# Combine rows kept in DRAM, two more weight slots, larger raw tiles, and a longer lead-in of idle products in a fused attention, soft mixture and feed-forward kernel

## The chip, the cores and the metric

The kernel runs on one core of a Trainium2 chip. The metric is device time in microseconds for one execution; lower is better. TensorE is called PE below, VectorE DVE, ScalarE ACT, GpSimd POOL, and SyncE, which issues most DMAs here, SP.

## What is computed

Three stages follow each other, all in float32 with a tight tolerance: causal attention with a cumulative bias (4 batches, 8 heads, 576 tokens, head width 64), a soft mixture of 8 experts over 2304 tokens, and a feed-forward block of width 2048.

```python
# attention, per head
cum = np.cumsum(np.maximum(s, 0.0), axis=-1)
scores = scale * q @ k.T + np.minimum(-(cum[:, None] - cum[None, :]), 0.0)   # causal mask
attn = softmax(scores);  x = attn @ v
# soft mixture: x is 2304 x 512
logits = x @ phi                                  # 2304 x 32 slots
slot_in = softmax(logits, axis=0).T @ x           # 32 x 512
slot_out[e] = relu(slot_in[e] @ w1[e]) @ w2[e]    # 8 experts, 4 slots each
c = softmax(logits, axis=1)                       # the combine rows
x = c @ slot_out
# feed-forward
h = x @ w_in
g = where(h >= 1, h, where(h <= -1, 0, (h + 1) ** 2 / 4))
out = g @ w_out
```

## The kernel before

**Attention.** The 32 heads are taken in 16 pairs, `pi`. The score rows of a pair are cut into row blocks `t`, and these into four groups `g` (`GROUPS`). For each group, `s_mm` makes the scores on PE in two steps: products of the raw q and k (tile `x`), and then products of the bias rows (tile `ext`, bf16). `maxima` takes masked row minima on DVE, `exps` the exponentials on ACT, `transp` transposes the result on PE, `evac_p` copies it out, and `pv` multiplies by v. Nothing is reordered by a scheduler: a list `plan` of (time, function) pairs is sorted once, and its order is the program order of every engine. One pair takes 12 units of plan time (`PLAN`, `GATE`, `PRE_AT` hold positions in it).

**Lead-in.** Before the first pair, DVE makes the running sum of s and splits it into three bf16 parts (tile `part`). ACT writes constant rows into `ext[0]` and `ext[1]` (line 255, four instructions each), and four small DMAs bring `part` into `ext[0]` (`ext_rows`, line 238, two issued by SP, two by ACT). `N_IDLE` = 7 products of the zeroed tile `ext[1]` with itself keep PE busy meanwhile (line 251). After each group of four pairs, that is, after each batch, `gate_parts` computes the softmaxes of the mixture; `c3` and `c3_tail` transpose the combine weights into 96 rows (value, value, rest) per token.

**Combine rows.** All 2304 columns of those rows stand in one SBUF tile, `cstack` (96 x 2304, 9 KB per partition), until the feed-forward stage reads them in blocks of 384 tokens.

**Weights.** The 64 parts of 512 KB of `w1` and `w2` are loaded into slots of 4 KB per partition. `slots` makes them: 16 "post" and `N_LEFT` = 12 "pre" slots exist from the start, and `PRE_AT` gives the 28 plan positions at which one load each is issued. When attention's own tiles are closed (`heads.close()`), 6 more "pre" and `N_TMP[0]` = 7 "tmp" slots come from their space, and 4 more when the last softmaxes are done. All later loads wait for a slot that an expert gives back (`release`). SP issues them in the order of `LOADS`. In the same stage `c3` of batch 2 and the softmaxes of batch 3 run.

**Raw tiles.** During attention, `w_in` (float64 in two int32 halves) is converted to float32 in chunks of 256 columns. `get` fetches one chunk of 256 KB (rows of 2 KB) into one of three tiles `st`; POOL (lines 665, 666) and DVE (690, 678) convert it.

**Feed-forward.** `h_part` multiplies a block of combine rows by `mst` (the slot outputs already multiplied by `w_in`), ACT and DVE make the activation and split it, and `o_part` makes nine products of 128x512 per unit. The very first product on combine rows is at line 1069.

## Time and profile before

| | |
|---|---|
| median of three runs | 453.62 us (453.22 to 454.09) |
| profiled execution, its own time | 454.85 us |
| its span, first to last instruction | 453.0 us |
| PE busy | 438.7 us, 97% |
| ACT, DVE, POOL busy | 338.2, 297.6, 57.2 us |
| HBM read, written | 66.93 MB, 6.93 MB |

The span is what the views of the trace show. The 1.85 us between it and the execution's own time lie around it. Busy time of PE is modelled from pipelined products, so that a full PE need not be at its peak.

### The profile page before, as it was taken

How to read it: one execution, taken by the hardware profiler on the slowest of the kernel's cores; microseconds unless marked ns; L12 is line 12 of the kernel's file. 1: busy time of each engine (PE TensorE's matmuls, PEld its weight loads, DVE VectorE, ACT ScalarE, POOL GpSimd, SP SyncE). 2: the span in 40 equal slices, each digit the busy share in tenths (PEclk: the TensorE clock that was granted, in tenths of full speed). 3: DMA queues.
4: the chain of work that ended last, by engine and by line, in shares of the span. 5: the costliest groups of instructions: out<-in, count | busy, mean ns of one | idle time of the engine just before them, and what ended most of it. 6: DMA issues, size and time to landing. Idle time of an engine off the chain costs nothing.

```text
span 453.0 us, 11875 instructions
## 1 busy us (share of the span) xinstructions
PE 438.7 (97%) x4406; PEld 335.3 (74%) x4406; DVE 297.6 (66%) x908; ACT 338.2 (75%) x916; POOL 57.2 (13%) x188
## 2 busy tenths in 40 slices
PE   8799999999999999998999999999999999999996
PEld 3577766776767677666666888888888888888884
DVE  5798988988898866300179897866555555545552
ACT  5899998998999895322379898976777767676772
POOL 2233413431430121000010000000000000000000
PEclk9999999999999999999999999999999999999999
DMA  3999898998787689899895550003001001001002
GB/s 80 245 278 249 250 260 258 279 290 212 211 225 232 176 263 302 300 398 408 302 375 213 200 192 17 0 2 140 1 0 69 1 0 71 1 1 71 0 1 70
DMA packets 30428, 75.24 MB, mean 166 GB/s; under 512 B 4514, under 2 KB 7138, under 8 KB 30370
## 3 DMA queue, kind: packets, MB, share of 16 engines
q1 hardware_dynamic: 30214, 74.34, 51.9%
q8 instruction: 35, 0.57, 0.5%
q14 instruction: 23, 0.19, 0.1%
q10 hardware_dynamic: 156, 0.14, 0.1%
HBM read 66.93 MB, written 6.93 MB: 163 GB/s over the span
## 4 chain that ended last, share of the span: by engine, by line
PE 91%; ACT 3%; DVE 3%; DMA 1%; issue 1%; SPq 0%; POOL 0%; ACTq 0%; POOLq 0%
PE o L992 14%; PE o L994 14%; PE o L993 13%; PE s L311 10%; PE s L422 8%; PE s L380 7%; PE s L457 4%; PE hp L960 3%; PE p L816 3%; PE p L785 3%; PE s L319 3%; PE s L414 3%; PE s L550 1%; PE s L739 1%; DVE g L974 1%
## 5 line engine op out<-in xcount | busy, mean ns | idle before, releaser
L992 PE MATMUL o<-wt,gh 128*128 128x512 f32 x288 | 113.0, 393 | 0.1
L993 PE MATMUL o<-wt,gh 128*128 128x512 f32 x288 | 112.1, 389 | 0.0
L994 PE MATMUL o<-wt,gl 128*128 128x512 f32 x288 | 112.1, 390 | 0.0
L370 ACT ACTIVATE P<-s,nm 128x256 f32<-128x256 f32 (+4 forms) x160 | 85.8, 557 | 10.5 <-DVE nm L325 9.6
L976 ACT CAST gh<-g 128x384 fp32r<-128x384 f32 x95 | 48.8, 514 | 48.6 <-DVE g L974 46.2
L982 DVE TENSOR_TENSOR gl<-g,gh 128x384 fp32r<-128x384 f32 x95 | 53.1, 559 | 40.8 <-ACT gh L976 40.7
L325 DVE CUSTOM_DVE_ANT_0 s<-s,tri 128x256 f32<-128x256 f32 (+4 forms) x160 | 73.8, 507 | 8.8 <-PE s L311 5.4
L974 DVE SCALAR_TENSOR_TENSOR g<-w,hp 128x384 f32<-128x384 f32 x95 | 52.5, 552 | 32.4 <-ACT w L965 31.9
L992 PEld LDWEIGHTS o<-wt,gh 128*128 128x128 f32 x288 | 54.2, 188 | 12.5 <-issue 1.5
L994 PEld LDWEIGHTS o<-wt,gl 128*128 128x128 f32 x288 | 54.1, 188 | 12.3 <-DVE gl L982 0.5
L993 PEld LDWEIGHTS o<-wt,gh 128*128 128x128 f32 x288 | 54.2, 188 | 7.6
L311 PE MATMUL s<-x 64*128 64x512 f32 (+3 forms) x256 | 56.5, 468 | 0.1
L964 ACT ACTIVATE w<-hp,half 128x384 f32<-128x384 f32 x95 | 54.8, 577 | 1.1 <-PE hp L916 1.1
L965 ACT ACTIVATE w<-w 128x384 f32<-128x384 f32 x95 | 49.9, 525 | 3.0
L406 ACT COPY pts<-s 128x384 f32<-128x384 f32 (+2 forms) x125 | 47.2, 471 | 0.8
L380 PE MATMUL s<-ident,P 64*128 64x64 f32 x800 | 42.3, 226 | 2.3 <-ACT P L370 2.2
L380 PEld LDWEIGHTS s<-ident,P 64*128 64x128 f32 x800 | 36.6, 139 | 10.4 <-issue 3.5
L370 ACT ACTIVATION_READ_ACCUMULATOR P<-s,nm 128x1 f32 x160 | 37.8, 236 | 0.0
L422 PE MATMUL s<-pts,v 128*64 128x512 f32 (+3 forms) x256 | 37.3, 433 | 0.1
L960 PE MATMUL hp<-cstack,mst 96*128 96x384 f32 x95 | 32.2, 340 | 1.1 <-DVE cv L177 0.9
L175 DVE TENSOR_SCALAR wt<-wt 128x512 int32<-128x512 int32 x20 | 9.1, 453 | 36.4 <-DMA wt<-in_w_out_dram 36.4
L311 PEld LDWEIGHTS s<-x 64*128 64x128 f32 x256 | 28.9, 193 | 4.8 <-issue 2.1
(177 smaller groups left out, 560.4 us busy)
## 6 DMA issues: line engine op xcount, KB each, us to landing
wt<-in_w_dram SPq DMA_DIRECT2D x64, 512.0 KB
x<-in_qkT_dram SPq DMA_DIRECT2D x32, 288.0 KB
wt<-in_w_out_dram SPq DMA_DIRECT2D x16, 512.0 KB
st<-in_w_in_dram SPq DMA_DIRECT2D x24, 256.0 KB
out_dram<-ob SPq DMA_DIRECT2D x17, 256.0 KB
v<-in_v_main_dram SPq DMA_DIRECT2D x16, 256.0 KB
w_in_f<-wif SPq DMA_DIRECT2D x4, 512.0 KB
wt<-w_in_f SPq DMA_DIRECT2D x4, 512.0 KB
```

Of the source, the lines that this page charges most:

```text
L311: T.matmul(out=o[h][:, off:off + n], lhsT=y[r, 0, c:c + 128], rhs=y[r, 1, 0:n], start=(k == 0), stop=(k == 1))
L325: V.tensor_tensor_reduce(out=sc, in0=sc, in1=mask[:, mask.shape[1] - n:], scale=-1.0 / SCALE, scalar=init, op0=ALU.add, op1=ALU.min, accum ...
L370: A.activation(out=out_, in_=in_, func=AF.Exp, bias=nm, scale=-1.0, accum_out=sm[:, k:k + 1])
L380: T.transpose(out=o[f][:, c:c + 64], in_=P[r], identity=ident[r, r])
L422: T.matmul(out=o[r, 128 * j:512], lhsT=vt[:, j, r], rhs=pts_t[pi][:, h, 512 * j:384 * j + 512], start=(j == 0), stop=(j == 3))
L964: A.activation(out=w, in_=hp, func=AF.Relu, bias=half, scale=0.5)
L965: A.activation(out=w, in_=w, func=AF.Square)
L974: V.scalar_tensor_tensor(out=g, in0=w, scalar=1.0, in1=hp, op0=ALU.min, op1=ALU.max)
L982: V.tensor_tensor(out=gl, in0=g, in1=gh.bitcast(F32), op=ALU.subtract)
L992: hh = lambda t: T.matmul(out=o_t[j][t], lhsT=gh[:, r[t]], rhs=wh[c], start=(c == 0), stop=False)
L993: hl = lambda t: T.matmul(out=o_t[j][t], lhsT=gh[:, r[t]], rhs=wl[c], start=False, stop=False)
L994: lh = lambda t: T.matmul(out=o_t[j][t], lhsT=gl[:, r[t]], rhs=wh[c], start=False, stop=(c == 15))
```

## The change

Six edits stand in one diff.

1. The lead-in has 15 idle products of 128x384 instead of 7 of 128x512. They read the mask tile `tri`, still zero in the columns used, and its memset moves ahead of that of `ext[1]` on POOL.
2. Fourteen more idle products (`WARM_0`: 5 of 128x384, 3 and 6 of 128x256) are put into the first pair: before the first transposes, between the transposes of its two heads, and after the scores of its last group.
3. In the first pair, the minima of group 1 are taken head by head.
4. The combine rows of a batch go into one tile `c_st` (96 x 576) and from there to DRAM (`c4`): by SP for batches 0 and 1, by ACT for batches 2 and 3. `c_load` brings them back in blocks of 384 tokens: blocks 0 and 1 just behind the one-element DMA `gate`, the others during the feed-forward stage. `idphi` moves from the lasting tiles to attention's own.
5. The space makes one more "pre" slot (13) and one more "tmp" slot (8). `PRE_AT` gets 29 positions, wider apart in the first two thirds of attention and closer in the last.
6. A raw tile holds two chunks (512 KB, rows of 4 KB). There are two such tiles, and each is asked for when the tile before the last has been read.

```diff
-N_IDLE = 7
+N_IDLE = 15
+WARM_0 = (5, 3, 6)
-N_LEFT = 12
+N_LEFT = 13
-N_TMP = (7, 4)
+N_TMP = (8, 4)
-PRE_AT = [3 * int(5 + 2.2 * _n) + 0.76 for _n in range(24)] + [171.76, 177.76, 183.76, 186.76]
+PRE_AT = [3 * int(5 + 2.55 * _n) + 0.76 for _n in range(19)] + [3 * int(52.3 + 1.1 * _n) + 0.76 for _n in range(10)]
 GATE = dict(
-    ... c3=27.64,
+    ... c3=27.64, c4=30.77,
...
-    cstack = const.tile([96, NTOK], F32R, name="cstack")
+    c_st = const.tile([96, S], F32R, name="c_st")
+    c_dram = w_dram.tile([96, NTOK], F32, name="c_rows")
...
                 nc.sync.dma_start(out=gate[0:1], in_=last[0:1, 0:1])
+                c_load(0, cs)
+                c_load(1, None)
...
-        stage = hpool("stage", 3)
+        stage = hpool("stage", 2)
...
         load_qk(0)
+        G.memset(tri, 0.0)
         G.memset(ext[1], 0.0)
...
-        idle = bank()
-        for _ in range(N_IDLE):
-            T.matmul(out=idle, lhsT=ext[1][:, 0, 0:128], rhs=ext[1][:, 0, 0:512], start=True, stop=True)
+        def idle_mm(out, n):
+            for _ in range(n):
+                T.matmul(out=out, lhsT=tri[:, 0:128], rhs=tri[:, 0:out.shape[1]], start=True, stop=True)
+        idle_mm(bank()[:, 0:384], N_IDLE)
...
+        idphi = hpool("idp", 1).tile([128, 4, D + NSLOT], F32, name="idphi")
...
+            if (pi, g) == (0, NG - 1):
+                idle_mm(o[0][:, 256:512], WARM_0[2])
...
-            for t, off in GROUPS[g]:
-                for k in heads_:
+            todo = [(k, *p) for p in GROUPS[g] for k in heads_]
+            for k, t, off in todo if pi else sorted(todo, key=lambda e: e[0]):
...
+            if (pi, g) == (0, 0):
+                idle_mm(o[0][:, 0:384], WARM_0[0])
...
+                if (pi, g, h) == (0, 0, 1):
+                    idle_mm(o[0][:, 256:512], WARM_0[1])
...
-                A.copy(out=cstack[:, S * b:S * b + 512], in_=ct[0:96])
+                A.copy(out=c_st[:, 0:512], in_=ct[0:96])
...
+            def c4():
+                (nc.sync if b < B - 2 else A).dma_start(out=c_dram[:, S * b:S * b + S], in_=c_st.bitcast(F32))
...
-            def get(n):
-                if n < len(wi_order):
-                    fb, k = wi_order[n]
-                    sts[n] = stage.tile([128, 2 * CHUNK], I32, tag="st", name="st")
-                    nc.sync.dma_start(out=sts[n], in_=w_in.bitcast(I32)[fb, :, 2 * CHUNK * k:2 * CHUNK * (k + 1)])
+            def get(m):
+                if 2 * m < len(wi_order):
+                    fb, k = wi_order[2 * m]
+                    sts[m] = stage.tile([128, 4 * CHUNK], I32, tag="st", name="st")
+                    nc.sync.dma_start(out=sts[m], in_=w_in.bitcast(I32)[fb, :, 2 * CHUNK * k:2 * CHUNK * (k + 2)])
...
                 exponent(n)
                 finish(n - 1)
+                if n and n % 2 == 0:
+                    get(n // 2 + 1)
                 yield
                 V.scalar_tensor_tensor(out=low, in0=lo, scalar=29, in1=hi, op0=ALU.logical_shift_right, op1=ALU.bitwise_or)
-                get(n + 2)
...
+    def c_load(j, p):
+        t = c_t[j] = p.tile([96, BLK], F32R, tag="cs", name="c_blk") if p else c_st[:, 0:BLK]
+        nc.sync.dma_start(out=t.bitcast(F32), in_=c_dram[:, BLK * j:BLK * j + BLK])
...
-        T.matmul(out=hp, lhsT=mst[0:96, 128 * c:128 * c + 128], rhs=cstack[0:96, BLK * j:BLK * j + BLK], start=True, stop=True)
+        T.matmul(out=hp, lhsT=mst[0:96, 128 * c:128 * c + 128], rhs=c_t[j], start=True, stop=True)
...
+    c_at = {16: 2, 24: 3, seq.index((3, 2)): 4, seq.index((4, 2)): 5}
     for i in range(1, len(seq) + 1):
+        if i in c_at:
+            c_load(c_at[i], cs2)
```

Where instructions move, the order on the engines shows it. On ACT, at the very start of the program, the rows of before are these (`ext_177` is `ext[0]`, `ext_188` is `ext[1]`; what an instruction waits for stands in brackets):

```order
L255 ACT_TABLE_LOAD
L255 ACTIVATE ext_177<-ones 6x576 [waits DVE_49]
L255 ACTIVATE ext_177<-ones 6x576 x3
L255 ACTIVATE ext_188<-ones 6x576 [waits PE_49,Pool_49]
L255 ACTIVATE ext_188<-ones 6x576 x3
L238 DMA ext_177<-part 3x1x576 [waits DVE_49,Activation_49]
L238 DMA ext_177<-part 3x1x576 [waits Activation_49]
```

And these are the rows of the change at the same place (`ext_181` is `ext[0]`, `ext_192` is `ext[1]`):

```order
L262 ACT_TABLE_LOAD
L262 ACTIVATE ext_181<-ones 6x576 [waits DVE_49]
L262 ACTIVATE ext_181<-ones 6x576 x3
L262 ACTIVATE ext_192<-ones 6x576 [waits Pool_49]
L262 ACTIVATE ext_192<-ones 6x576 x3
L241 DMA ext_181<-part 3x1x576 [waits DVE_49,Activation_49]
L241 DMA ext_181<-part 3x1x576 [waits Activation_49]
```

The order is the same, but the fifth activation no longer waits for PE, since the idle products don't read `ext[1]` any more.

On DVE, in the first pair, the minima of groups 0 and 1 stand like this before (each `ISA s,nm` is one masked minimum, group 1's are those of 384 and 128 columns, one of each per head):

```order
L325 ISA s,nm<-s,tri 128x512
L325 ISA nm 128x1
L325 ISA s,nm<-s,tri 128x384
L325 ISA nm 128x1
L325 ISA s,nm<-s,tri 128x384
L325 ISA nm 128x1
L325 ISA s,nm<-s,tri 128x128
L325 ISA nm 128x1
```

In the change they stand like this:

```order
L334 ISA s,nm<-s,tri 128x512
L334 ISA nm 128x1
L334 ISA s,nm<-s,tri 128x384
L334 ISA nm 128x1
L334 ISA s,nm<-s,tri 128x128
L334 ISA nm 128x1
L334 ISA s,nm<-s,tri 128x384
L334 ISA nm 128x1
```

The first head's minimum over 128 columns moved ahead of the second head's over 384.

On SP, at the end of the expert weights, the rows of before are these:

```order
L159 DMA wt<-in_w_dram 128x1024 x38
L159 DMA wt<-in_w_out_dram 128x1024 x2
L141 DMA gate<-wt 1x1
L159 DMA wt<-w_in_f_155 128x1024 x2
L159 DMA wt<-in_w_out_dram 128x1024 x2
L159 DMA wt<-w_in_f_156 128x1024 x2
```

In the change, these stand there:

```order
L163 DMA wt<-in_w_dram 128x1024 x38
L163 DMA wt<-in_w_out_dram 128x1024 x2
L143 DMA gate<-wt 1x1
L789 DMA c_blk<-c_rows 96x384
L789 DMA c_st<-c_rows 96x384
L163 DMA wt<-w_in_f_159 128x1024 x2
L163 DMA wt<-in_w_out_dram 128x1024 x2
L163 DMA wt<-w_in_f_160 128x1024 x2
```

The two loads of combine rows stand between `gate` and the next weights, so they are issued only when the last expert weight has landed, for which `gate` waits.

## Rows read from the trace of the kernel before

**Rows 1.** Stretches: length; PE, PEld, DVE, ACT, POOL busy; granted clock; DMA share; GB/s.
```profile
20.00:170.00 150.00, 150.00 (x2192) 107.28 (x2191) 130.03 (x551) 137.51 (x481) 45.25 (x154) 1.00 0.86 244
158.00:160.00 2.00, 2.00 (x34) 1.45 (x32) 1.17 (x6) 1.99 (x9) 0.37 (x2) 1.00 0.17 8
186.00:192.00 6.00, 5.89 (x113) 3.78 (x117) 0.46 (x2) 2.84 (x8) 0.00 (x0) 1.00 0.76 242
194.00:220.00 26.00, 22.96 (x531) 16.60 (x527) 0.00 (x0) 6.29 (x21) 0.00 (x0) 1.00 1.02 407
249.00:440.00 191.00, 191.00 (x915) 159.98 (x914) 118.87 (x220) 143.47 (x283) 1.24 (x2) 1.00 0.13 46
```

**Rows 2.** PE in order of time, lead-in: start, length, instruction, idle before it.
```profile
1.85 3.17 PE L251 MATMUL s<-ext 128*128 128x512 bf16 x7 [1.85 <-POOL ext L246]
5.10 4.51 PE L311 MATMUL s<-x 64*128 64x512 f32 x8
...
10.77 0.55 PE L311 MATMUL s<-ext 64*128 64x512 bf16 x4
...
12.96 1.04 PE L380 MATMUL s<-ident,P 64*128 64x64 f32 x16 [1.10 <-ACT P L370]
...
15.06 0.27 PE L380 MATMUL s<-ident,P 64*128 64x64 f32 x1 [0.46 <-ACT P L370]
15.97 0.71 PE L380 MATMUL s<-ident,P 64*128 64x64 f32 x15 [0.64 <-ACT P L370]
```

**Rows 3.** PE groups by shape, 5 to 8 us: busy, mean ns of one.
```profile
L311 PE MATMUL s<-x 64*128 64x512 f32 x4 | 3.2, 1137 | 0.1
```

**Rows 4.** The same view, 25 to 28 us.
```profile
L311 PE MATMUL s<-x 64*128 64x512 f32 x4 | 1.3, 629 | 0.0
```

**Rows 5.** Chain that ended last, lead-in: start, length, what.
```profile
7.67 0.26 SPq L238
...
8.71 2.19 DMA exts<-part
```

**Rows 6.** Who waited for whom, 0 to 17 us: total, times, longest.
```profile
ACT ext L255 <- PE s L251: 0.5, 1, 0.5
```

**Rows 7.** ACT and DVE in order of time, first pair, group 1.
```profile
13.04 0.60 DVE L325 CUSTOM_DVE_ANT_0 s<-s,tri 128x384 f32<-128x384 f32 x1
...
13.56 0.33 DVE L325 CUSTOM_DVE_ANT_0 s<-s,tri 128x128 f32<-128x128 f32 x1
...
13.98 0.58 ACT L370 ACTIVATE P<-s,nm 128x384 f32<-128x384 f32 x1 [0.50 <-DVE nm L325]
```

**Rows 8.** POOL in order of time, first raw chunk.
```profile
17.10 0.43 POOL L665 TENSOR_SCALAR wif<-st 128x256 f32<-128x256 f32 x1 [0.61 <-DMA st<-in_w_in_dram]
```

**Rows 9.** SP in order of time: issues of weight loads and of `gate`.
```profile
178.71 0.67 SPq L159 DMA_DIRECT2D wt<-in_w_dram  x1
...
185.88 0.33 SPq L159 DMA_DIRECT2D wt<-in_w_dram  x1
...
211.46 0.33 SPq L159 DMA_DIRECT2D wt<-in_w_dram  x1
...
221.54 0.68 SPq L141 DMA_DIRECT2D gate<-wt  x1
222.32 0.34 SPq L159 DMA_DIRECT2D wt<-w_in_f  x1
```

**Rows 10.** Who waited for whom, SP's queue, 150 to 260 us.
```profile
SPq L159 <- DVE new L753: 5.7, 1, 5.7
```

**Rows 11.** ACT in order of time, last softmaxes.
```profile
180.33 0.62 ACT L605 CAST cstack<-s 96x512 fp32r<-96x512 f32 x1
181.62 0.34 ACT L536 ACTIVATE dn<-dn 128x160 f32<-128x160 f32 x1 [0.67 <-DVE dn L522]
```

**Rows 12.** Instructions on output tile `ob`: count, ns min/median/max.
```profile
L1010 ACTq DMA_DIRECT2D out_dram<-ob x1: 378/378/378, 449.4 to 449.4; - x1
```

**Rows 13.** PE in order of time, first product on combine rows.
```profile
226.99 0.81 PE L1069 MATMUL hp<-cstack,mst 64*128 64x384 f32 x2
```

More of the change, by code (lines that the diff above doesn't have):

```diff
@@ L74 @@
 GATE = dict(
-    d1=13.08, c0=15.51, d2=15.75, c1=15.81, d3=18.75, d4=18.76, c2=20.99, d5=21.75, d6=25.27, c3=27.64,
+    d1=13.08, c0=15.51, d2=15.75, c1=15.81, d3=18.75, d4=18.76, c2=20.99, d5=21.75, d6=25.27, c3=27.64, c4=30.77,
 )
@@ L212, in attention_softmoe_ffn_kernel @@
         v_t.append(fx.tile([128, 5, 128], F32, name="v1"))
-        idphi = const.tile([128, 4, D + NSLOT], F32, name="idphi")
         su_ctx = ExitStack()
@@ L265, in attention_softmoe_ffn_kernel @@
         ext_rows(1, exts, [nc.sync] * 4)
-        G.memset(tri, 0.0)
         G.affine_select(out=tri[:, 384:512], in_=tri[:, 384:512], compare_op=ALU.is_ge, fill=-BIG, base=0,
@@ L348, in maxima @@
             heads_ = (h,) if len(GROUPS[g]) == 1 else (0, 1) if h == 0 else ()
-            for t, off in GROUPS[g]:
-                for k in heads_:
-                    nm = column(2 * t + k)
-                    nm_t_.setdefault((pi, g, k), []).append(nm)
-                    masked_min(o[k][:, off:off + 128 * (t + 1)], tri, BIG, nm)
+            todo = [(k, *p) for p in GROUPS[g] for k in heads_]
+            for k, t, off in todo if pi else sorted(todo, key=lambda e: e[0]):
+                nm = column(2 * t + k)
+                nm_t_.setdefault((pi, g, k), []).append(nm)
+                masked_min(o[k][:, off:off + 128 * (t + 1)], tri, BIG, nm)
         def exps(pi, g, h):
@@ L604, in c3 @@
                     c_rows(ct[:, 128 * t:128 * t + 128], 128, t)
-                A.copy(out=cstack[:, S * b:S * b + 512], in_=ct[0:96])
+                A.copy(out=c_st[:, 0:512], in_=ct[0:96])
             def c3_tail(ct):
                 c_rows(ct, 64, 4)
-                A.copy(out=cstack[:, S * b + 512:S * b + S], in_=ct[0:96])
+                A.copy(out=c_st[:, 512:S], in_=ct[0:96])
+            def c4():
+                (nc.sync if b < B - 2 else A).dma_start(out=c_dram[:, S * b:S * b + S], in_=c_st.bitcast(F32))
             if b == B - 2:
-                last_c.append(c3)
-            parts = dict(d1=d1, c0=c0, c1=c1, d2=d2, c2=c2, d3=d3, c3=c3, d4=d4, d5=d5, d6=d6, st=st, c2_div=c2_div,
+                last_c.extend((c3, c4))
+            parts = dict(d1=d1, c0=c0, c1=c1, d2=d2, c2=c2, d3=d3, c3=c3, c4=c4, d4=d4, d5=d5, d6=d6, st=st, c2_div=c2_div,
                          c2_parts=c2_parts)
@@ L624, in attention_softmoe_ffn_kernel @@
             for n, t in GATE.items():
-                if n == "c3" and b == B - 2:
+                if n in ("c3", "c4") and b == B - 2:
                     continue
@@ L652, in parts @@
                 fb, k = wi_order[n]
-                w = sts[n].rearrange("p (n two) -> p n two", two=2)
+                w = sts[n // 2][:, 2 * CHUNK * (n % 2):2 * CHUNK * (n % 2 + 1)].rearrange("p (n two) -> p n two", two=2)
                 return fb, k, flat[:, CHUNK * k:CHUNK * (k + 1)], w[:, :, 0], w[:, :, 1]
-            def get(n):
-                if n < len(wi_order):
-                    fb, k = wi_order[n]
-                    sts[n] = stage.tile([128, 2 * CHUNK], I32, tag="st", name="st")
-                    nc.sync.dma_start(out=sts[n], in_=w_in.bitcast(I32)[fb, :, 2 * CHUNK * k:2 * CHUNK * (k + 1)])
+            def get(m):
[3 more added lines that the diff above has]
+                    nc.sync.dma_start(out=sts[m], in_=w_in.bitcast(I32)[fb, :, 2 * CHUNK * k:2 * CHUNK * (k + 2)])
             def exponent(n):
@@ L739, in warm @@
                 T.matmul(out=idle[:, 0:128], lhsT=ident, rhs=ident, start=True, stop=True)
-        last_c[0]()
+        for f in last_c:
+            f()
         for n, k in zip(("d1", "d2", "d3", "d4"), WARM_T):
@@ L765, in attention_softmoe_ffn_kernel @@
     soT = ex.tile([128, 4, NSLOT], F32, tag="soT", name="soT", bufs=1)
+    cs = ctx.enter_context(tc.tile_pool(name="cs", bufs=1))
+    c_t = {}
+    def c_load(j, p):
+        t = c_t[j] = p.tile([96, BLK], F32R, tag="cs", name="c_blk") if p else c_st[:, 0:BLK]
+        nc.sync.dma_start(out=t.bitcast(F32), in_=c_dram[:, BLK * j:BLK * j + BLK])
     w_free += slots(tmp_ctx, "tmp", N_TMP[1])
@@ L805, in last_rows @@
         yield
-        c = S * (B - 1)
-        for a, b, m in ((c, c + 512, ct), (c + 512, c + S, tail)):
-            A.copy(out=cstack[0:64, a:b], in_=m[0:64])
-            A.copy(out=cstack[64:96, a:b], in_=m[0:32])
+        for a, b, m in ((0, 512, ct), (512, S, tail)):
+            A.copy(out=c_st[0:64, a:b], in_=m[0:64])
+            A.copy(out=c_st[64:96, a:b], in_=m[0:32])
+        A.dma_start(out=c_dram[:, S * (B - 1):], in_=c_st.bitcast(F32))
         yield
@@ L902, in attention_softmoe_ffn_kernel @@
     mst = fin[0].tile([96, DFF], F32R, name="mst")
+    cs2 = ctx.enter_context(tc.tile_pool(name="cs2", bufs=2))
     gens = conv_g
@@ L1068, in attention_softmoe_ffn_kernel @@
     for k in (slice(0, 64), slice(64, 96)):
-        T.matmul(out=hp0[:, 0:BLK], lhsT=mst[k, 0:128], rhs=cstack[k, 0:BLK], start=(k.start == 0), stop=(k.start > 0))
+        T.matmul(out=hp0[:, 0:BLK], lhsT=mst[k, 0:128], rhs=c_t[0][k], start=(k.start == 0), stop=(k.start > 0))
     m_pair(m_2, 256)
```

## The prediction

> **What bounds the kernel now.** I read the stretches first, since a share over the whole span mixes stages with different limits. In attention PE is busy 150.00 of 150 us, and in the feed-forward stage 191.00 of 191, with DMA at a share of 0.13 [rows 1]. In both, PE's own products set the time, and the change leaves those products alone. In the expert stage between them PE is busy 22.96 of 26 us, while the DMA share is 1.02 at 407 GB/s [rows 1]: there the weights set the pace. What is left is the start. PE has something to do from 1.85 us on, but the first products that follow each other without a wait begin with the transposes at 15.97 [rows 2]. So three places can move: the lead-in, the 40 us of weights, and any new wait that the change puts into the full stretches.
>
> In the lead-in I compared one shape at two times. A product of x with 512 columns takes 1137 ns on average early and 629 ns later [rows 3, 4]. The granted clock reads 1.00 in all these rows, so the reader should go by the durations: they stand nearly two to one, as 1.2 and 2.4 GHz do. PE ran at the lower level from 1.85 until about 10.8 us, when the bias products began, although it had work almost without a break [rows 2]. Beside it runs a second chain, through ACT's constant rows (end at 7.67), SP's issue of the bias rows behind them, and the copy of `part` to DRAM [rows 5].
>
> **The change, part by part.** *Constant rows.* Before, ACT waits 0.5 us for the idle products, because they read `ext[1]`, which ACT then writes [rows 6]. In the change they read `tri` and that wait is gone. Everything behind the constant rows moves up by 0.5 us: bias rows, the copy to DRAM, the next pair's x.
>
> *Idle products.* Seven of 512 columns took 3.17 us [rows 2], 0.45 us each, so one of 384 columns is some 0.34 us at the lower level, and fifteen are 5.1 us. They begin earlier, behind a smaller memset, and PE then goes straight on to the products of x. If this turns the clock by the time these run, they take about half of the 5.67 us that they take now (5.10 to 10.77 [rows 2]) and end near 9. The bias products then wait for their rows. No view shows when those land. The last of these DMAs is issued after 7.98 on SP (7.67 + 0.26 + 0.05) and somewhat later on ACT; the copy of `part`, far larger, takes 2.19 us from issue to landing [rows 5]. So now they are there by some 10.2 to 10.6, and 0.5 earlier in the change: 9.7 to 10.1. Against 10.77 that is 0.67 to 1.07 gained; I take 0.7, since the ACT issue is the later one.
>
> *Minima by head.* ACT stands idle 0.50 us before the exponentials of group 1, while DVE does the other head's 384 columns [rows 7]. In the change the first head's second minimum, 0.33 long, takes the place at 13.04 and ends about 13.4; ACT is free at 13.48, so nearly all of that wait goes: 0.45. The second head's minima then end before ACT gets to them. ACT is on the path here (PE waits 0.64 for its P at 15.97 [rows 2]).
>
> *Idle products in the first pair.* Five of 384 and nine of 256 columns: at the higher level half of 0.34, that is 0.17, and 0.11 each, 1.9 us in all. PE waits 1.10, 0.46 and 0.64 us at these places [rows 2], 2.2 together, so they fit, at nothing. If the waits shrink first, the excess is at most some 0.3. The clock was at its upper level there anyway. Lead-in: -0.7 - 0.45 = **-1.15 us**, bounds +0.3 - 0.7 = -0.4 and -1.07 - 0.45 - 0.2 = -1.7.
>
> *The 29th load.* One load is 524,288 B, 1.29 us at 407 GB/s. It now goes in attention, where the DMA engines have room: at 158 to 160 us they are busy 0.17 of the time [rows 1], all early slots being full. It is missing later from a stage at a share of 1.02: -1.29.
>
> *Combine rows out.* Each batch is 96 x 576 x 4 B = 0.22 MB. Those of batches 0 and 1 go in attention, under PE. Those of 2 and 3 fall into the weights, 0.54 us each at 407 GB/s: +1.08. ACT issues them in order. The first stands between the copy of the rows (end 180.95) and the exponential at 181.62, for which DVE's input comes only then [rows 11]; an issue takes 0.38 on ACT where it is undisturbed [rows 12], so the 0.67 us idle covers it. Without that cover it costs 0.38 in the softmaxes.
>
> *The 8th temporary slot.* SP issues the last load into attention's space at 178.71, then waits 5.7 us for DVE and goes on at 185.88 [rows 9, 10]. From 186 to 192 the DMA share is 0.76 [rows 1]: 6 x 0.24 = 1.44 us of nothing. One more load in front of that hole fills up to 1.29 of it. I take 1.0, since the first batch written fills some too; bounds 0 and 1.29. Weights: -1.29 + 1.08 - 1.0 = **-1.2 us**, bounds -0.2 and -1.5.
>
> *Combine rows back.* Blocks 0 and 1 are asked for behind `gate`, from 222.32 on [rows 9], with an empty queue ahead. At 2.19 us, the nearest row [rows 5], block 0 is there by 224.6; PE needs it at 226.99 [rows 13]. Nothing, covered by 2.4 us. The weights behind slip by 0.8 us of issue and 0.7 of transfer; no view shows PE waiting for them in the feed-forward stage. The other blocks come under 191 us of full PE.
>
> *Raw tiles.* The first is twice as large, and POOL waited 0.61 us for its half [rows 8]. Later ones are asked for four steps ahead instead of three. I take nothing, as POOL is off the path. Were every one of the twelve late by that 0.61 on the path, it would cost 7.
>
> **Sum:** -1.15 - 1.2 = -2.35. The profiled execution, 454.85 = 453.0 + 1.85, would be 452.5. The median of the runs lies 1.23 below it, and the stages are the same there: 453.62 - 2.35 = **451.3 us**.
>
> **The rivals.** *A. The clock turns no earlier.* Then fifteen products at 0.34 hold PE until 6.1 to 6.9, the products of x take their 5.67 us behind them, and the bias products begin at 11.8 to 12.6, 1.0 to 1.85 later than now; say +1.2. With the minima, +0.75, and with the weights -0.45 in all: 453.2. For it speaks that 8.9 us of work did not turn the clock before 10.8 [rows 2]; against it that this work had a break before and while x arrived, and the new one has none. The Trainium skill (TensorE: Matmul & The Clock Gate, Part 1) says that half rate is the default and sustained activity lifts it, and that the moment depends on where a kernel starts in a window that runs freely; by that rule this rival can happen in one run and not in the next. The trace agrees that PE starts at the lower level; it has one turn, so the spread is shown by no row.
>
> *B. The hole in the weights stays*, because the slots behind it, not the queue, set it. The extra slot earns nothing, the written rows eat most of the 29th load: -0.2, with the lead-in -1.35: 452.3. For it: the wait for DVE is as long as before [rows 10]. Against it: the share of 0.76 is a queue run dry, and one more load lengthens it.
>
> *C. Slower: block 0 comes late.* A weight load under the full queue takes from 211.46 to 221.54, 10.1 us, to land [rows 9]. If block 0 took that from 222.32, it would land at 232.4, and PE would stand 5.4 us at its first product: 453.62 - 2.35 + 5.4 = 456.7. It decides from some 3.3 us behind 226.99 on. Against it: `gate` waits until the last weight is there, so that nothing is left ahead.
>
> **How the numbers follow.** The forecast holds 0.62, A 0.13, B 0.15, C 0.05; 0.05 is left for what I don't see. A measurement of this kernel can tell 0.2%, 0.91 us: below 452.71 is faster, above 454.53 slower. The forecast alone spans 450.4 to 453.0 by its bounds. The range holds it and B whole and most of A; below it goes 0.5 further, for a before that starts in an unluckier phase than the profiled one: 449.9 to 453.3. Faster: the forecast (0.61 of it), B, and a little of A: 0.78. Same: most of A and the rest, 0.14. Slower: C and half of the unseen, 0.08.
>
> **What would show it.** PE: products of x in half their time and bias products near 10 us; ACT: no wait before the constant rows of `ext[1]` nor before group 1's exponentials; the transposes of 15.97 near 14.8. DMA: a share near 1 at the place of 186 to 192, and `gate` some 2.3 us earlier. Wrong would be: products of x still at 1137 ns, the hole unchanged, or a wait of PE for `c_blk`.

## The result and the profile after

The change made the kernel slower: 456.53 us median against 454.12, a ratio of 1.0056 with a 95% interval of 1.0033 to 1.0079. (In the ratios, here and below, an execution more than 1.5% above the fastest of its kernel is left out; the medians count all.) The forecast was 451.3. Single executions spread more than before (454.63 to 461.59 against 452.61 to 456.40). The profiled one took 458.90, with a span of 457.04. It is one of the slower ones, 2.4 us above the median, so what it lost in attention is more than the usual loss; two further profiles of the same kernel below lost less there.

Where the 4.0 us of the two spans lie, by marks that stand in PE's order of time in both traces (the first product of P and v of the first and of the sixteenth pair, the first layer-1 product, the first product into `m`, the end):

```
                     first P v   to 16th pair   to layer 1   to m     to the end
before               22.02       151.73         12.36        39.39    227.53
changed              20.52       156.32         12.36        40.85    227.00
difference           -1.50       +4.59           0.00        +1.46    -0.53
```

So the lead-in did win, and attention gave back three times as much in this execution. The same stretches as in [rows 1], and two around 48 us (length; PE, PEld, DVE, ACT, POOL busy; granted clock; DMA share; GB/s):

```profile
20.00:170.00 150.00, 147.52 (x2126) 105.75 (x2128) 128.40 (x545) 133.44 (x469) 46.21 (x157) 0.99 0.86 242
38.00:48.00 10.00, 7.70 (x124) 5.60 (x120) 8.22 (x34) 8.90 (x32) 4.54 (x15) 1.00 1.02 307
48.00:53.00 5.00, 4.85 (x35) 3.70 (x35) 1.76 (x6) 1.43 (x4) 2.71 (x9) 0.69 0.82 233
158.00:160.00 2.00, 2.00 (x42) 1.34 (x40) 2.00 (x10) 1.67 (x6) 0.00 (x0) 1.00 0.97 248
186.00:192.00 6.00, 5.27 (x64) 2.54 (x56) 3.23 (x14) 0.43 (x2) 0.32 (x1) 0.82 0.94 339
194.00:220.00 26.00, 23.55 (x562) 17.13 (x558) 0.00 (x0) 8.14 (x25) 0.00 (x0) 1.00 1.01 385
249.00:440.00 191.00, 191.00 (x910) 159.19 (x909) 121.22 (x225) 144.92 (x287) 1.23 (x2) 1.00 0.14 49
```

Two things are new. In attention PE is no longer busy throughout: 2.5 us are missing, and the clock is not 1.00. And the DMA engines, which had a share of 0.17 at 158 to 160 and 0.76 at 186 to 192, are at 0.97 and 0.94 over the same stretches. But attention ends 3.08 us later here, so the same work stands 3.08 us further on: from 0.11 us ahead of the first layer-1 product the six microseconds read 0.87 at 272 GB/s (189.08 to 195.08) where they read 0.76 at 242, and the earlier dip is 0.54 at 162 to 164. Both holes are shallower than before, and not filled. The chain that ended last shows the place of the loss (start, length, what):

```profile
38.35 9.66 DMA x<-in_qkT_dram
48.01 0.14 issue
48.15 1.31 PE s L318 x3
```

and PE in order of time around it, with the idle time ahead of an instruction and its releaser:

```profile
45.04 0.66 PE L389 MATMUL s<-ident,P 64*128 64x64 f32 x16
48.15 1.34 PE L318 MATMUL s<-x 64*128 64x512 f32 x3 [2.44 <-DMA x<-in_qkT_dram]
```

The first half of the x of the fifth pair is asked for at 38.35 and lands 9.66 us later (the other half at 48.69); PE stands 2.44 us for it, and runs at the lower clock behind that: 0.69 over 5 us means 5 x 0.31 x 2 = 3.1 us at half speed, some 1.55 us lost (the fall ends at 53.3, just past the stretch). 2.44 + 1.55 = 4.0 of the 4.59. What stood ahead of that x on SP's queue:

```profile
34.30 0.36 SPq L676 DMA_DIRECT2D st<-in_w_in_dram  x1
34.76 0.38 SPq L688 DMA_DIRECT2D w_in_f<-wif  x1
35.19 0.42 SPq L163 DMA_DIRECT2D wt<-in_w_dram  x1
35.87 1.04 SPq L245 DMA_DIRECT2D v<-in_v_main_dram  x1
36.96 0.65 SPq L246 DMA_DIRECT2D v<-in_v_tail_dram  x1
37.66 0.59 SPq L163 DMA_DIRECT2D wt<-in_w_dram  x1
38.35 1.31 SPq L234 DMA_DIRECT2D x<-in_qkT_dram  x2
```

Four transfers of 512 KB, 0.29 MB of v and the first half of x (0.29 MB) are 2.7 MB; at the 307 GB/s of the stretch 38 to 48 that is 8.8 us. That is most of the 9.66, and the DMA share is 1.02 while x waits: what x waits for is a full queue.

The lead-in, with the rows that answer to [rows 2, 3]:

```profile
1.32 4.68 PE L256 MATMUL s<-tri 128*128 128x384 bf16 x15 [1.32 <-POOL tri L249]
5.93 2.25 PE L318 MATMUL s<-x 64*128 64x512 f32 x8
...
9.29 0.37 PE L318 MATMUL s<-ext 64*128 64x512 bf16 x1 [0.41 <-DMA ext<-part]
10.36 0.37 PE L318 MATMUL s<-ext 64*128 64x512 bf16 x2 [0.70 <-DMA ext<-part]
...
12.29 0.47 PE L389 MATMUL s<-ident,P 64*128 64x64 f32 x8
...
14.87 0.71 PE L389 MATMUL s<-ident,P 64*128 64x64 f32 x16
```

```profile
L318 PE MATMUL s<-x 64*128 64x512 f32 x4 | 1.6, 641 | 0.0
```

The products of x take 641 ns where they took 1137 [rows 3], and the transposes of 15.97 [rows 2] stand at 14.87. Behind attention there is SP in order of time at `gate`, and PE at its first product on the rows:

```profile
223.24 0.68 SPq L143 DMA_DIRECT2D gate<-wt  x1
223.97 0.37 SPq L789 DMA_DIRECT2D c_blk<-c_rows  x1
224.43 0.39 SPq L789 DMA_DIRECT2D c_st<-c_rows  x1
```

```profile
231.53 0.81 PE L1095 MATMUL hp<-c_blk,mst 64*128 64x384 f32 x2
```

Block 0 lands at 226.28, 2.31 us behind its issue (a landing is read here as the last update of its semaphore ahead of the next issue on the same one), and is used 5.2 us later. `gate` is 1.7 later than before, although attention ended 3.08 later, so the stage of the weights became shorter.

### The profile page after: what moved, and what is told of

The parts are those of the page before. It is cut to its first block, busy times and chain, and to the rows that moved or that the text cites. A ratio compares the mean times of both kernels' runs of the same rounds, so it can differ in the third digit from the quotient of the medians.

```text
span 457.0 us, 11909 instructions
## 1 busy us (share of the span) xinstructions
PE 443.3 (97%) x4428; PEld 338.7 (74%) x4428; DVE 297.6 (65%) x908; ACT 338.6 (74%) x916; POOL 57.4 (13%) x188
## 4 chain that ended last, share of the span: by engine, by line
PE 90%; DMA 4%; ACT 3%; DVE 1%; issue 1%; ACTq 0%; SPq 0%
PE o L1018 14%; PE o L1019 14%; PE o L1020 14%; PE s L318 10%; PE s L435 7%; PE s L389 6%; PE s L470 4%; PE hp L986 4%; PE p L810 4%; PE p L841 3%; PE s L328 3%; PE s L427 2%; DMA x<-in_qkT_dram 2%; DMA wt<-in_w_out_dram 1%; ACT ext L262 1%
## 5 line engine op out<-in xcount | busy, mean ns | idle before, releaser
L1008 DVE TENSOR_TENSOR gl<-g,gh 128x384 fp32r<-128x384 f32 x95 | 53.0, 558 | 40.9 <-ACT gh L1002 40.7
L1000 DVE SCALAR_TENSOR_TENSOR g<-w,hp 128x384 f32<-128x384 f32 x95 | 52.5, 553 | 32.8 <-ACT w L991 32.3
L389 PE MATMUL s<-ident,P 64*128 64x64 f32 x800 | 42.4, 227 | 0.0
L435 PEld LDWEIGHTS s<-pts,v 128*64 128x64 f32 x256 | 17.2, 137 | 17.2 <-issue 14.7
```

What stands on the lines that cost most here:

```text
L389: T.transpose(out=o[f][:, c:c + 64], in_=P[r], identity=ident[r, r])
L435: T.matmul(out=o[r, 128 * j:512], lhsT=vt[:, j, r], rhs=pts_t[pi][:, h, 512 * j:384 * j + 512], start=(j == 0), stop=(j == 3))
L1000: V.scalar_tensor_tensor(out=g, in0=w, scalar=1.0, in1=hp, op0=ALU.min, op1=ALU.max)
L1008: V.tensor_tensor(out=gl, in0=g, in1=gh.bitcast(F32), op=ALU.subtract)
```

## The experiments

The theories have letters in the expectations: T, the raw tiles' 512 KB transfers make x late; C, the clock falls by chance; D, the rows hold SP; then Q, the early weight loads make x late, and F, the rows lie in a full DMA stream. For each kernel the table gives the median, that of the kernel before beside it on the same chip, and the ratio with its interval; and of the profiled execution the time from the first to the sixteenth pair, and for x of the fifth pair when it landed and when PE first used it (a pair's first product can begin when the first half of x, that of its first head, is there, so a use can stand ahead of the landing; the second product needs the other half).

```
kernel          median  before  ratio (95%)               1st to 16th  x lands  used
before                                                     151.73       45.59   46.30
changed         456.53  454.12  1.0056 (1.0033 to 1.0079)  156.32       48.69   48.15
after2          456.32  453.87  1.0075 (1.0046 to 1.0103)  152.68       47.26   46.16
raw2k           456.69  453.87  1.0041 (1.0016 to 1.0065)  157.42       48.12   47.04
leadin          454.62  453.87  1.0000 (0.9972 to 1.0027)  155.39       47.67   46.48
rows            454.90  453.87  1.0022 (0.9999 to 1.0044)  152.48       47.67   47.02
before_late     453.73  453.95  0.9996 (0.9975 to 1.0018)  152.22       42.43   45.42
leadin_late     452.75  453.95  0.9990 (0.9970 to 1.0011)  151.05       41.42   44.71
after_late      455.50  453.95  1.0034 (1.0012 to 1.0057)  153.51       41.59   45.90
raw2k_late      455.65  453.95  1.0035 (1.0004 to 1.0066)  158.75       40.91   44.73
fit             453.73  453.88  0.9988 (0.9958 to 1.0018)  151.11       40.57   44.62
fit_ahead       453.53  453.88  0.9966 (0.9937 to 0.9994)  151.33       40.78   44.69
rows_only       456.92  453.88  1.0059 (1.0021 to 1.0096)  151.82       46.12   46.35
leadin_late2    452.40  453.88  0.9960 (0.9934 to 0.9987)  151.05       41.21   44.73
writes_only     457.02  454.07  1.0064 (1.0033 to 1.0094)  151.65       45.36   46.47
rows_ahead      456.70  454.07  1.0046 (1.0015 to 1.0078)  151.32       45.73   45.64
after_fit       455.43  454.07  1.0034 (1.0013 to 1.0054)  151.95       41.40   45.47
```

**1. The change in its parts.** `raw2k` is the changed kernel with the raw tiles of before:

```
-        stage = hpool("stage", 2)
+        stage = hpool("stage", 3)
...
-                if n and n % 2 == 0:
-                    get(n // 2 + 1)
...
+                get(n + 2)
```

> The changed kernel with the raw tiles of before (three of 2 KB a partition, asked for at the old step). Theory T (the 512 KB raw transfers delay a pair's x in attention): no wait of PE for x between 38 and 50 us, no fall of the granted clock there; the 2.4 us of waiting and half of the 3.4 us at the lower level come back, 4.1 in all, so a span near 453 and a time near 454.1 - 0.5 to - 2, faster than before by up to 2 us. Theory C (the clock falls because the earlier start of the idle products shifts the kernel, whatever the raw tiles do): falls stay, 456 to 457. Theory D (the rows written to DRAM hold SP and the weights): attention is mended or not, but PE still ends its expert stage some 5.7 us behind the gate instead of 2.8, time 455 to 456.

Theory T fell: PE waited 2.2 us for the same x, the clock fell behind it (0.77 over 45 to 60 us), and 456.69 is within the noise of the changed kernel. The larger raw tiles are not what makes x late.

`leadin` is the kernel before with N_IDLE, WARM_0, the mask tile and the minima by head of the change, and nothing else.

> The kernel before with the lead-in alone: fifteen idle products from the mask tile, fourteen in the first pair, minima by head. Theories T and D: attention starts 0.9 to 1.5 us earlier, as in the changed kernel's profile (its first products of P and v at 20.52 against 22.02, the second pair's at 30.75 against 31.62), and nothing later takes it back: 0.9 us faster than before, some 453.2. Theory C: the clock falls once or twice in attention or behind it, each time for some 3.4 us, and the time is 1 to 2 us above before, 455 to 456.

The first product of P and v stands at 20.50, 1.5 us ahead, yet the median did not fall. The profiled execution took 155.39 us from the first to the sixteenth pair: x of the fifth pair landed at 47.67, 2.1 us later than in the kernel before, for a PE that was 1.5 us earlier. So T's and D's "nothing takes it back" fell, and for C speak two falls of the clock (near 189 and 233 us), but the 3.7 us in attention came without one. Where they begin, the rows show. A raw tile lands late, POOL waits for it, and the wait goes on through DVE, which takes the tile from POOL ahead of minima of the fourth pair, and through ACT:

```profile
39.31 0.43 POOL L675 TENSOR_SCALAR wif<-st 128x256 f32<-128x256 f32 x1 [1.85 <-DMA st<-in_w_in_dram]
```

```profile
40.28 0.42 DVE L700 SCALAR_TENSOR_TENSOR low<-st 128x256 int32<-128x256 int32 x1 [2.31 <-POOL st L676]
```

```profile
42.10 0.58 ACT L376 ACTIVATE P<-s,nm 128x384 f32<-128x384 f32 x1 [2.34 <-DVE nm L331]
```

Then PE meets x of the fifth pair late; the chain that ended last goes over that DMA:

```profile
39.83 7.84 DMA x<-in_qkT_dram
47.67 0.14 issue
47.81 0.40 PE s L315
```

The table of waits has only 0.2 us of this for PE, since the rest stands inside products that read as busy.

`rows` is the changed kernel without the lead-in and with raw tiles of 2 KB: rows through DRAM, the two slots and the new PRE_AT are left.

> The kernel before with the combine rows through DRAM, the two more weight slots and the new times of the early loads alone; lead-in and raw tiles as before. Theory T: the gate some 1.2 us earlier against the end of attention, the time 0.5 to 1.2 us below before, 453.0 to 453.6. Theory D: SP stands some 5 us for a row transfer, PE waits longer for weights in the expert stage, 0.5 to 2 us above before. Theory C says nothing of it: same as before within 0.3.

1.0 us slower by the median, inside D's range, and SP did stand 4.9 us for a row transfer. But D's reason fails: in the profiled execution `gate` was issued at 219.43, 2.1 earlier than before. Instead x of the fifth pair was late (PE waited 0.8 for it).

`after2` is the changed kernel again.

> The changed kernel once more, to see whether its loss lies at the same place. Theory T: PE waits 1 to 4 us for x of the fourth pair near 45 us again, and the clock falls behind that wait; 456.5 by the median. Theory C: the clock falls at other places than before, and no wait for x need stand ahead of it. In runs without a fall the span is 452.5 to 453.6, as the earlier runs with a mean clock of 0.999 and 1.000 show.

The same x came late, landing at 47.26 (1.1 us behind its first use), and no fall of the clock followed it; one stood at 11.5 us, ahead of the first pair. The clock falls at different places, but x of the fifth pair is late in all four kernels. That gave a new theory, Q: the first 47 us of attention are paced by DMA, and a PE that starts earlier finds x missing.

**2. Moving the early weight loads.** The first four of PRE_AT, asked for ahead of that x, go to a later place; in the kernel before and the lead-in:

```
-PRE_AT = [3 * int(5 + 2.2 * _n) + 0.76 for _n in range(24)] + [171.76, 177.76, 183.76, 186.76]
+PRE_AT = sorted([3 * int(5 + 2.2 * _n) + 0.76 for _n in range(4, 24)] + [123.76, 135.76, 144.76, 156.76, 171.76, 177.76, 183.76, 186.76])
```

and in the two others the same with `range(4, 19)` and 111.76, 123.76, 132.76, 141.76. These are positions in the plan, not microseconds.

> The kernel before with the first four of the early weight loads (those asked for ahead of x of the fifth pair) moved to 100 to 140 us. Theory Q (DMA, not PE, paces the first 47 us of attention, and x of the fifth pair lands behind these loads): x of the fifth pair lands 2 to 5 us earlier than 45.59; PE had it 0.72 us ahead of its use, so nothing is won at that place: the same as before within 0.5 us. Theory C (falls of the clock make the loss, wherever they happen by chance): the same too. Slower by some 1 us only if the four loads are missing later.

> The lead-in alone, with the same four loads moved. Theory Q: x of the fifth pair lands before 44, PE has no wait between 38 and 50 us, the first products of P and v of pairs 1 to 8 all stand some 1.5 us ahead of before (20.5, 30.1, 39.7, 49.6, ...), and the time is 1.0 to 1.5 us below before, and 1 to 2 below the lead-in alone. Theory C: the falls come by chance as before, the time equals that of the lead-in alone within 0.5, about 454.6.

> The changed kernel with its first four early loads moved to 100 to 130 us. Theory Q: no wait for x and no fall of the clock between 38 and 55 us, attention ends 1.0 to 1.5 ahead of before instead of 3.1 behind; time 452 to 453.5, 3 to 4.5 below the changed kernel. Theory C: 456 as the changed kernel, with the falls elsewhere.

> The same with raw tiles of 2 KB. Theory Q with raw tiles that cost nothing of their own: the same as the kernel with 4 KB tiles and late loads, within 0.5 us. If the 512 KB transfers cost something besides (the expert stage took 39.2 us with them without a fall of the clock, and 37.9 and 38.4 without them), this one is 0.5 to 1.3 us faster.

As Q has it, x landed at 40.9 to 42.4 in all four, and moving the loads earned nothing where PE was not early (`before_late`). With the lead-in it did. The stretches 20 to 45 and 45 to 60 us of `leadin`:

```profile
20.00:45.00 25.00, 24.27 (x348) 17.54 (x347) 20.05 (x87) 22.02 (x79) 8.50 (x27) 1.00 0.85 246
45.00:60.00 15.00, 14.77 (x198) 10.16 (x196) 12.83 (x51) 13.28 (x47) 5.91 (x18) 1.00 0.94 255
```

and of `leadin_late`:

```profile
20.00:45.00 25.00, 25.00 (x380) 18.82 (x379) 21.96 (x95) 23.58 (x84) 9.59 (x31) 1.00 0.75 214
45.00:60.00 15.00, 15.00 (x215) 10.73 (x215) 14.14 (x60) 14.15 (x49) 5.47 (x19) 1.00 0.96 259
```

348 products became 380 in the same 25 us, and 198 became 215. So a stretch that reads as 97 or 98% busy did 8% less. (Some products can be missing from a trace; the marks agree: from the first product of the fourth pair to that of the eighth, `leadin` took 45.30 us and `leadin_late` 41.60.) The Trainium skill (Perfetto Trace Analysis, Identifying the Most-Contended Engine) says that the busy share of matmuls is no good measure of how close a kernel is to roofline, as pipelined instructions look smaller in a trace, and that of weight loads is one; the trace agrees, PEld is 17.54 against 18.82, 7% less, where PE is 24.27 against 25.00. The ratio of 0.9990 did not settle the gain in time, since two of the twelve executions were above 455.

`after_late` and `raw2k_late` missed Q's numbers by 2 to 3 us. Their traces show why: x of the thirteenth pair, near the new places of the four loads, landed 0.9 and 0.7 us behind its first use (and x of the fourteenth 1.0, with a wait of 1.8 us and a fall of the clock at 145 us, in `raw2k_late`), and in `after_late` PE then stood 1.9 us in the feed-forward stage for `mst`.

**3. Better places, and the rows alone.** `fit` is `raw2k` with the four loads at the plan positions 63.76, 102.76, 117.76 and 153.76, where x had come 3 us or more ahead. `fit_ahead` also asks for the two blocks ahead of `gate`:

```
-                nc.sync.dma_start(out=gate[0:1], in_=last[0:1, 0:1])
                 c_load(0, cs)
                 c_load(1, None)
+                nc.sync.dma_start(out=gate[0:1], in_=last[0:1, 0:1])
```

> Lead-in, combine rows through DRAM and the two slots together, raw tiles of 2 KB, and the first four early loads moved to places where x of the next pairs came 3 us or more ahead of its use (near 62, 94, 107 and 136 us), since at 111 to 142 they only made x of the 13th and 14th pair late. Theory Q (late x is the whole loss): no wait for x anywhere, 452 to 453.3. Theory F (what is read and written for the combine rows lies in a DMA stream that is full from 158 us to the copies into mst near 246 us, and PE waits for mst there): PE meets mst late, 0.5 to 2 us of waiting near 246 us, and a time of 454 to 455.5 in spite of an attention that ends 1.5 us earlier than before.

> The same, with the two blocks of combine rows asked for ahead of gate instead of behind it, so that they land while SP waits for gate, where the DMA engines run dry. Theory F: the copies into mst land 24.4 to 24.8 us behind gate's issue instead of 25.6 to 26.6, and the time is 0.7 to 1.3 us below the kernel that asks behind gate. Theory Q: the same within 0.4.

No wait for x was left in either: there Q holds. `fit` lies between the two expectations by its median, 2.97 us below `raw2k` (each beside its own kernel before; 2.4 by the ratios, with some 1.8 either way), from which it differs in the places of four loads alone. Of `fit_ahead` the expected mechanism failed: the copies into `mst` landed 26.3 us behind `gate`, not 24.4 to 24.8, and at the same time as in `fit` (242.79 and 242.85); the two times are within each other's noise.

`rows_only` is the kernel before with the rows through DRAM: N_LEFT 12, N_TMP 7 and PRE_AT as before.

> The kernel before with the combine rows through DRAM and nothing else: no further slots, the early loads at their old times, lead-in and raw tiles as before. Theory F: 1.08 us of written rows and 0.7 to 1.5 us of rows read behind gate, part of the first in the hole at 186 to 192, so 0.7 to 2 us slower than before, 454.7 to 456, with PE waiting for mst. Theory Q: the same as before within 0.5, 453.5 to 454.5.

3.0 us slower: theory F, with more than it asked. The end of the chain that ended last, near the start of the feed-forward stage:

```profile
229.62 10.72 DMA wt<-in_w_in_dram
...
241.68 6.95 DMA mst<-m_lo
248.63 0.09 issue
248.72 0.41 PE hp L975
```

PE's wait there, and the stretch behind it, in `rows_only`:

```profile
PE hp L975 <- DMA mst<-m_lo: 2.1, 1, 2.1
```

```profile
250.00:253.00 3.00, 3.00 (x9) 2.40 (x8) 2.30 (x4) 1.60 (x4) 0.24 (x1) 0.50 0.28 55
```

and the same wait in the kernel before:

```profile
PE hp L960 <- DVE cv L177: 0.9, 1, 0.9
```

The wait was there before, under another name. The third copy into `mst` landed at 246.27, 0.14 us ahead of PE's restart at 246.41. DVE's conversion ended at 246.29, so this trace alone doesn't tell the two apart; but in all seven profiles in which PE stood 0.7 us or more here it restarts 0.09 to 0.14 us behind the third copy, whichever releaser is named. So DMA sets the end of that wait in both kernels, and what is put into the full stream is paid. In `rows_only` `gate` is 1.5 us later, `mst` 2.4 (248.63), PE's restart 2.31. Behind it PE does 9 products in 3 us at a clock of 0.50 (0.98 over 242 to 250): 3.0 + 0.3 us at half speed, 1.65 lost. 2.31 + 1.65 is most of the 4.3 by which the span is longer.

`leadin_late2` is `leadin_late` once more.

> The lead-in with the late loads once more, as its median (452.75) and its ratio of means (0.999) disagree on how much it wins. Theory Q: a median of 452.5 to 453, 1.0 to 1.4 below before, with single runs above 455 where the clock fell. If those falls are as frequent as in the lead-in alone, the ratio is 1.000.

452.40, 0.996: with the first four loads moved, the lead-in wins 1.2 and 1.5 us by the two medians, 0.5 and 1.8 by the two ratios, of which only the second is clear of its interval. It is the fastest version found, and beats both kernels.

**4. The price of the rows, and the raw tiles.** `writes_only` keeps `cstack` in SBUF and writes the rows out besides; `rows_ahead` is `rows_only` with the two blocks ahead of `gate`; `after_fit` is the changed kernel with the PRE_AT of `fit`.

```
+            def c4():
+                (nc.sync if b < B - 2 else A).dma_start(out=c_dram[:, S * b:S * b + S], in_=cstack[:, S * b:S * b + S].bitcast(F32))
```

> The kernel before, with the combine rows also written to DRAM, and used from SBUF as before: nothing is read back. If the writes take the full DMA stream for 1.08 us as forecast, gate and the copies into mst come 1.1 later and PE, which already waited 0.9 there, waits 2.0: 1 us slower without a fall of the clock, 455, and with the fall that a longer wait brings in most runs 456.5. If the reads behind gate are what costs, 454 to 454.4.

> Combine rows through DRAM alone, with the two blocks asked for ahead of gate, into the stretch in which the DMA engines run dry (share 0.71 at 220 to 226 us when they are asked for behind it). If the reads' place matters, the copies into mst land 0.7 to 1.3 us earlier than the 248.5 of the kernel that reads behind gate, and the time is 0.7 to 2 us below its 456.9. If only the bytes matter, 456.5 to 457.

> The changed kernel itself, with nothing but its first four early loads moved (63.76, 102.76, 117.76 and 153.76 of the order's steps in place of 15.76 to 36.76). If raw tiles of 4 KB cost nothing: as with 2 KB, 453.5 to 453.8, some 2.8 us below the changed kernel. If they cost something of their own: 454.3 or more, with x of some pair late behind a 512 KB transfer.

The writes without the reads cost as much as both (457.02), and the reads' place makes no difference that can be told (456.70). So, within the some 2 us that these intervals leave, the reads behind `gate` were rightly taken as nearly free, and the writes were not. `after_fit` is 0.0046 of the ratio above `fit`, about 2 us, with half-widths of 0.003 and 0.002: raw tiles of 4 KB cost something where x is no longer late (it was late for no pair of `after_fit`, so not by the way that was expected). Between the changed kernel and `raw2k` it is 0.0015 to 0.0034, between the two late ones nothing; its size stays open.

The profiled execution of `writes_only` (454.93) was one of its fastest, so it was profiled again, and the changed kernel too:

> The written rows alone, a second look. If its typical loss is the late copies into mst: PE waits 1.5 to 2.5 us there near 247 us and the clock is down for 3.4 us behind it, a time of 456.5 to 457.5, and attention ends where it ended before (the first layer-1 products at 186.2). If it is x behind the write on SP's queue: attention ends 1 to 4 us later, with PE waiting for x of the pairs behind 75 and 118 us.

> The same kernel, a third look, with the same two expectations.

> The changed kernel, a third look: x of the fifth pair lands at 47 to 49 us and PE waits for it; a wait for mst near 246 us of 0.8 to 2 us only if the first did not already make PE late.

They came out at 458.62, 452.79 and 453.85. The first lost its time in attention (155.53 us from first to sixteenth pair, 151.08 in the second):

```profile
PE s L312 <- DMA x<-in_qkT_dram: 1.3, 2, 1.0
```

x landed behind its first use for the fifth, sixth and seventh pair, of which the loads stand ahead of the first write, at 77.85 us. So that execution's loss is not made by the writes in front of it, and neither expectation is borne out. In `after_look3` x of the fifth pair was again late (0.91 us behind its first use), without a fall of the clock, and the first to the sixteenth pair took 153.00 us.

## Why the prediction was wrong

**Lead-in, -1.15: the gain was there, its way to the end was not.** The first P and v product came 1.50 us earlier, inside -0.4 to -1.7. Within it, the constant rows moved nothing: SP issues the copy of `part` at 8.79 (8.71 before [rows 5]), since SP's first issues wait for DVE's `part` as before; the last bias rows that PE waits for landed at 10.23, not 9.7 to 10.1. The clock did the work, with the products of x at 641 ns; the minima filled ACT's wait as forecast. The step that failed is the first paragraph's "PE's own products set the time" in attention. PE's busy time of 150.00 of 150 [rows 1] seemed to say so, but the same line has the DMA engines at a share of 0.86, and x of the fifth pair landed 0.7 us ahead of its use; that of the sixth already landed 0.38 us behind its first product, at 56.47 against 56.09. This cover was in no term; moving PE 1.5 us earlier used it up. What came late was not x alone: in `leadin` a raw tile was, and held DVE for 2.31 us. x also landed later in itself, at 46.9 to 48.7 in the five profiles with the lead-in and the early loads in their place; why is not shown, and three profiles of `writes_only`, without the lead-in, spread from 44.7 to 47.3. In five profiles with the lead-in and the early loads in their place the first to the sixteenth pair took 152.7 to 157.4 us, in five with the loads moved to good places 151.05 to 151.95. This is shown by the traces of `leadin` against `leadin_late`, which differ in four entries of PRE_AT, and by the times of `raw2k` against `fit`. What it took in the changed kernel's profile: 2.44 of waiting, 1.55 of clock.

**The clock's fall** was in no term and no rival. A single wait of about 2 us brought one in every profile that has such a wait (2.44 us in the changed kernel, 2.2 in `raw2k`, 2.1 in `rows_only`, 2.2 in `rows_ahead`, 1.9 in `after_late`, 1.8 in `raw2k_late`); the wait of 1.2 for `mst` in `writes_only` brought none. Between these sizes it went either way: behind 1.42 us at 232.51 in `leadin` and 1.12 at 227.07 in `fit` the clock fell, behind 1.47 at 198.59 in `after2` and 1.49 at 197.98 in `after_look3` it did not. Around the last softmaxes, whose waits are the same in every kernel (12.36 us in all), it fell in eight of the twenty profiles and in the others not: in the changed kernel the clock is 0.82 over 186 to 192 and 0.92 over 192 to 200, 2.2 + 1.3 us at half speed, 1.7 lost, against the +1.46 of the expert stage; before it was 1.00 [rows 1]. Rival A, that the clock turns no earlier, occurred in part in one of twelve profiles with the lead-in: in `raw2k` the first two products of x still took 1217 and 1161 ns, without a loss. The moment of the turn does differ between executions of one order of instructions. The lead-in of before had products of x with 512 columns at 1137 ns in the kernel before, and at 641 and 718 in `rows_ahead` and `writes_look1`. The Trainium skill's rule on this (TensorE: Matmul & The Clock Gate, Part 1, on a moment that depends on where the kernel starts) agrees.

An early turn alone is not kept. In the three profiles that have the old lead-in and turned before the bias products, the clock fell again at 11.7, 12.5 and 14.5 us (`rows_ahead`, `writes_look1`, `before_late`), and the first P and v product stands at 21.24 to 21.91. With the new lead-in it fell in one of twelve (`after2`, at 11.5, 21.40 instead of 20.52); the other eleven have 20.41 to 20.52. So the idle products inside the first pair, which the prediction took at nothing because the clock was up there anyway, may be what holds it up; no run has them alone.

**29th load and 8th slot, -1.29 - 1.0.** Not contradicted: `rows` against `rows_only` is the two slots with their load times, -2.0 by the medians and -1.7 by the ratios, with some 2 us either way. Rival B failed: the hole is shallower (0.87 for 0.76), and in the 16 us around the first layer-1 product (from 8 us ahead of it) the DMA engines moved 346 GB/s where they moved 295, 0.8 MB more, 2.0 us at 407 GB/s. The sum for the weights as a whole, -1.2 at `gate`, also came out near: from the first layer-1 product to `gate`'s issue it is 32.3 to 34.0 us in the ten profiles with rows and slots, 33.7 to 35.4 in the five with neither, 1.1 less by the means.

**Combine rows out, +1.08: mis-sized.** `rows_only` measured +3.0 and `writes_only` +2.9 by the medians (+2.7 and +2.9 by the ratios, at least 1.0 and 1.5 by their intervals). Part of the reason is shown: the forecast charged the two writes' bytes once and closed the sum at `gate`, but the stream is full beyond it up to the copies into `mst`, and PE's wait for these doubles and takes the clock with it (`rows_only`, `rows_ahead`). The cover on ACT held as far as foreseen:

```profile
183.41 0.62 ACT L618 CAST c_st<-s 96x512 fp32r<-96x512 f32 x1
184.06 0.37 ACTq L625 DMA_DIRECT2D c_rows<-c_st  x1
184.71 0.34 ACT L549 ACTIVATE dn<-dn 128x160 f32<-128x160 f32 x1 [0.68 <-DVE dn L535]
```

Not foreseen were SP's own waits in the changed kernel, 5.6 us for ACT's rows at a write in attention and 5.4 for a row transfer's landing in the expert stage, with loads queued behind both:

```profile
SPq L625 <- ACT c_st L618: 5.6, 1, 5.6
SPq L163 <- DMA c_rows<-c_st: 5.4, 1, 5.4
```

How much of the 2.9 us lies there, and how much in the `mst` wait, stays open: three profiles of `writes_only` at 452.8, 454.9 and 458.6 show three different courses. In them `gate` is issued 34.6, 35.1 and 36.3 us behind the first layer-1 product, against 35.4 before and 36.7 and 38.3 in `rows_only` and `rows_ahead`: for the writes alone no trace shows the forecast 1.08 at `gate`, and the cost of 2.9 rests on the times.

**Combine rows back, 0.** Right: 2.31 us to land against the 2.19 assumed, 5.2 us of cover. Rival C failed. The sentence that no view shows PE waiting for the weights behind them was wrong for `mst`; the wait stood in the view of waits under DVE's name.

**Raw tiles, 0.** POOL waited 3.27 for the first instead of 0.61 [rows 8]. Up to 2 us by `fit` and `after_fit`, not told from nothing in the other two pairs. The reason given, that POOL is off the path, does not hold: in `leadin`, with the tiles of before, a late tile held POOL, DVE and ACT in turn, and PE's transposes just ahead of the fifth pair stand at 45.87, where `leadin_late` has them at 44.21.

Added up by runs: lead-in 0 where it should have been -1.15, rows +3.0 where +1.08 stood, slots -2.0 where -2.29 stood, raw tiles 0 to 2. That is +1 to +3 against the +2.4 measured; each of these terms is uncertain by 1 to 2 us, so the sum agrees but proves little.

## What to carry to other kernels

An engine that reads as fully busy may be less than a microsecond from waiting. Before an edit that starts a stage earlier, list for each transfer in it, those of side work included, when it landed and when it was first used, and take the smallest of these as the cover that the edit spends; where it is too small, move other transfers out of the way in the same edit. A stream that is full is paid up to its last user, so follow it beyond the wait at which the sum would close.

## Not expected of the hardware

The profile put the wait for `mst` down to DVE in the kernel before (0.9) and to the DMA in the experiment (2.1), though by the times of landing and restart the same copy ended both. And executions of one program differ more in attention than PE's busy time suggests: in three profiles of `writes_only`, with the same instructions in the same order, the first to the sixteenth pair took 151.08, 151.65 and 155.53 us, while PE was busy 150.00, 149.91 and 148.62 of the 150 us from 20 to 170.
